# Later stages for the first weight unit, one engine for each PSUM bank of y, and T3 in front of T4: a fused attention and two-MLP kernel on one NeuronCore

## Chip, core and metric

The kernel runs on one core of a Trainium2 chip. The metric is the device time in microseconds of one execution. A profiled execution gives its own time and a span from the first to the last instruction; the sums below are made against that execution.

## What is computed

Linear attention with random features over 4 batches, 8 heads, 576 tokens of 64 values, and then two MLPs on the 2304 tokens of 512 values that the attention gives. All is float32.

```
phi(x): h = einsum('bhsd,md->bhsm', x, omega) - sum(x*x)/2 ; exp(h - max(h)) / sqrt(m)
kv  = einsum('bhsm,bhsd->bhmd', phi(k), v) ;  z = sum(phi(k), axis=2)
out = einsum('bhsm,bhmd->bhsd', phi(q), kv) / (einsum('bhsm,bhm->bhs', phi(q), z) + 1e-06)
x = out as (2304, 512)
MLP 1:  h = x @ w_in (512 x 2048);  g = max(h, 0) + alpha * min(h, 0);  x = g @ w_out
MLP 2:  h = x @ w_in (512 x 2048);  r = max(h, 0);  x = (r * r) @ w_out
```

## The kernel before, in words

**Attention.** `seq` is 18 tiles of 128 tokens of the keys and then 18 of the queries. `k_step(i)` for key tile i puts on the engines: the load of a later key and value tile (SP), the kv products of tile i-3 (TensorE, L560), the projection of tile i on omega (TensorE, L514, into a PSUM tile h, of which there are two), the sums of squares (L521), and for tile i-1 the maximum and the bias (VectorE, L527, L533, L534) and eight exponentials (ScalarE, L539, which read h). GpSimd copies the values (L604) and squares the keys (L503). So the projection of tile i writes the h that the exponentials of tile i-2 have read. Three last key steps are interleaved with the first query steps (`q_step`), which go on alone after them.

**Weights.** MLP weights come as int64 words; `Raw` loads one (L115, issued by GpSimd) and a generator, `made`, takes it in small *stages* through ScalarE scaling (`scale_high` L125, `scale_low` L128), VectorE shifts and merges (L132, L135), a GpSimd add (L137), then splits it in two float32r parts (ScalarE cast L212, VectorE rest L215), adds Strassen sums (L151) and writes the result to DRAM (`keep` L218, `keep3` L237) for later blocks, which read it back (`read`, L396). Each call of `onward` runs one stage. Weight *unit* 0 is asked for after k_step(1) (its two loads of 512 KB are issued then); from key step `MAKE_K` on, each key step ends with one stage of it, and so do the first two interleaved query steps. Stages 15 to 17 of unit 0 are empty. Later `upto` runs stages up to a number that a table names.

**MLP 1.** Three blocks of 768 tokens, each with eight *turns* (one pair of 128-column weight slices each). A turn of a block after the first does seven Strassen products (`pair`, L746) in the order 1, 2, 6, 5, 7, 4, 3, and between them, as `FILL` says, the parts of the second matmul (`mm2`, L930) of the turn before, which add into y: six PSUM banks of 512 columns, holding four pieces of 768 columns, so that banks 1 and 4 hold two pieces of 256. L771 on ScalarE makes `gh`, the rounded activation that mm2 reads, from c, which VectorE bends (L789). After a block's last mm2, `evacuate` (L948) copies y to x; this stands in the first turn of the next block, piece by piece as `COMPLETE` frees banks. At a block's end the table `NEXT` places the preparation of the next block's operands: differences T1 to T4 (L414; T1 and T3 in tile ta, T2 and T4 in tile tb), casts (ScalarE L421, xh) and rests (VectorE L424, xl). Product 7 reads T3, product 4 reads T4. MLP 2 follows with its own order.

**Order.** TensorE, VectorE, ScalarE and GpSimd execute in exactly the order in which the code issues; each is one queue, so an instruction that waits holds up all behind it. SyncE's order of transfers is chosen by the framework. Two engines that read one PSUM bank are put one after the other by the framework's semaphores.

Of the kernel before, what the change touches and what calls it, by code (L numbers as in the profile page):

```python
# [26 lines left out]
KC = DM // P  # L27
# [6 lines left out]
HB = NB // 2  # L34
NPAIR = NF // 2
QW = 2 * P
MAKE_K = 2

ZEROS = (8, 4, 4)

# [14 lines left out]
def tile_performer_moe(ctx, tc, qt, kt, qn, kn, vn, omt, w1i, w1o, al, w2i, w2o, out):  # L55
    nc = tc.nc
# [27 lines left out]
    B11, B21, B22, T4, T1, T2, T3 = range(7)  # L84
# [282 lines left out]
    def onward(most, blk):  # L367

        ask(most, blk)
        next(making[0])  # L370
# [6 lines left out]
    def ask(most, blk):  # L377

        limit[0], room[0] = most, blk
        if not making:  # L380
            making.append(made())
            next(making[0])
        fetches[0]()
# [42 lines left out]
    def as_it_is(_, n):  # L426
# [9 lines left out]
            11: [(rest, T4), (cast, B22)], 12: [(rest, B22)]},  # L436
        1: {-4: [(difference, T1)], -2: [(difference, T2)],
            1: [(cast, B11)], 2: [(rest, B11), (cast, B21)], 3: [(rest, B21), (cast, T2)],
            4: [(rest, T2), (cast, T1)], 5: [(rest, T1), (difference, T4)], 6: [(difference, T3), (cast, T4)],
            7: [(cast, T3), (rest, T4)], 8: [(rest, T3), (cast, B22)], 9: [(rest, B22)]},  # L440
    }


# [6 lines left out]
    def attention():  # L450
        with ExitStack() as ac:
# [235 lines left out]
            for i in range(NT):  # L687
                k_step(i)
                if i == 1:
                    ask(1, BLOCKS - 1)  # L690
                elif i >= MAKE_K:
                    onward(1, BLOCKS - 1)
# [243 lines left out]
    def cuts(c):  # L936

        a0 = c * NB
        while a0 < (c + 1) * NB:
            a1 = min((c + 1) * NB, (a0 // 512 + 1) * 512)  # L940
            yield a0, a1
            a0 = a1

    def evacuate(k, y, rows):

        for n, (c, a0, a1) in enumerate((c, a0, a1) for c in range(KC) for a0, a1 in cuts(c)):
            if a0 // 512 in rows:
                (nc.scalar.copy, nc.vector.tensor_copy)[n % 2](  # L948
                    out=x[:, k, c, a0 - c * NB:a1 - c * NB],
                    in_=y[a0 // 512][:, a0 % 512:a0 % 512 + a1 - a0])  # L950

# [31 lines left out]
    for n, (layer, k, turn, p) in enumerate(plan):  # L983
# [10 lines left out]
        for m, got in enumerate(steps, DRAINED if n == 0 else 0):  # L994
# [25 lines left out]
            for rows in full:  # L1020
                evacuate(ended, y, rows)
# [8 lines left out]
        for rows in full:  # L1030
            evacuate(ended, y, rows)
# [281 lines left out]
```

## Time and profile before

| | |
|---|---|
| median of 3 runs | 890.82 us (888.67 to 893.08) |
| profiled execution | 893.57 us, of which the span is 891.8 us |
| mean granted TensorE clock over the span | 0.994 |
| TensorE matmul busy | 881.9 us (99% of the span) |
| VectorE / ScalarE / GpSimd busy | 676.5 / 480.4 / 169.7 us |

How to read it: TensorE is the engine that sets the time, since it is busy almost throughout. But a busy matmul row counts a matmul at half clock as busy too, so the idle time alone does not tell what can be had. The profiled execution is 2.75 us above the median and 0.49 us above the slowest of the three runs.

### The profile page before, as it was taken

How to read it: one execution, taken by the hardware profiler on the slowest of the kernel's cores; microseconds unless marked ns; L12 is line 12 of the kernel's file. 1: busy time of each engine (PE TensorE's matmuls, PEld its weight loads, DVE VectorE, ACT ScalarE, POOL GpSimd, SP SyncE). 2: the span in 40 equal slices, each digit the busy share in tenths (PEclk: the TensorE clock that was granted, in tenths of full speed). 3: DMA queues.
4: the chain of work that ended last, by engine and by line, in shares of the span. 5: the costliest groups of instructions: out<-in, count | busy, mean ns of one | idle time of the engine just before them, and what ended most of it. 6: DMA issues, size and time to landing. Idle time of an engine off the chain costs nothing.

```text
span 891.8 us, 18473 instructions
## 1 busy us (share of the span) xinstructions
PE 881.9 (99%) x7328; PEld 837.0 (94%) x7328; DVE 676.5 (76%) x1078; ACT 480.4 (54%) x965; POOL 169.7 (19%) x192
## 2 busy tenths in 40 slices
PE   8999999999999999999999999999999999999998
PEld 5998889999998999998999999999999999999998
DVE  4767987999987778898787975668845688657674
ACT  5688886677665466475565643334523254333432
POOL 5553232444412222321323100000000000000000
PEclk9899999999999999999999999999999999999999
DMA  7445224789954899947999965767687687876763
GB/s 259 149 133 200 77 84 154 255 288 321 283 211 188 292 377 400 402 163 264 362 413 394 386 238 183 256 253 276 224 302 253 210 310 254 278 258 222 301 247 141
DMA packets 86902, 228.82 MB, mean 257 GB/s; under 512 B 6688, under 2 KB 19360, under 8 KB 81824
## 3 DMA queue, kind: packets, MB, share of 16 engines
q1 hardware_dynamic: 77248, 192.21, 59.9%
q0 software_dynamic: 9216, 33.56, 11.6%
q10 hardware_dynamic: 352, 1.87, 0.6%
q8 instruction: 58, 0.95, 0.4%
q14 instruction: 28, 0.23, 0.1%
HBM read 170.47 MB, written 57.15 MB: 255 GB/s over the span
## 4 chain that ended last, share of the span: by engine, by line
PE 54%; DVE 2%; ACT 0%; issue 0%; DVEq 0%; ACTq 0%
PE h L746 16%; PE sumb L746 10%; PE suma L1113 9%; PE sumc L1113 8%; PE y L930 8%; PE sumb L1113 3%; DVE xl L424 1%; PE h L1113 0%; DVE c L789 0%; DVE ms L215 0%; DVE c L784 0%; DVE wf L151 0%; DVE ta L414 0%; ACT gh L771 0%; DVE gl L795 0%
## 5 line engine op out<-in xcount | busy, mean ns | idle before, releaser
L746 PE MATMUL h<-xh,w 128*128 128x384 f32 x1040 | 294.7, 336 | 0.0
L746 PEld LDWEIGHTS h<-xh,w 128*128 128x128 f32 x1040 | 190.8, 188 | 2.5
L930 PE MATMUL y<-gh,w 128*128 128x512 f32 (+1 forms) x768 | 175.6, 337 | 1.4 <-ACT gh L771 1.4
L746 PE MATMUL h<-xl,w 128*128 128x384 f32 x520 | 174.7, 336 | 0.4 <-DVE xl L424 0.3
L930 PEld LDWEIGHTS y<-gh,w 128*128 128x128 f32 x768 | 131.0, 188 | 13.6 <-ACT gh L771 2.4
L137 POOL TENSOR_TENSOR wf<-x 128x512 int32<-128x512 int32 x64 | 86.2, 1347 | 240.7 <-issue 56.8
L930 PE MATMUL y<-gl,w 128*128 128x512 f32 (+1 forms) x384 | 103.4, 337 | 0.0
L746 PEld LDWEIGHTS h<-xl,w 128*128 128x128 f32 x520 | 97.7, 188 | 3.7 <-DVE xl L424 1.1
L1127 ACT CAST gh<-g 128x768 fp32r<-128x768 f32 x72 | 56.5, 831 | 81.2 <-PE suma L1113 38.9
L746 PE MATMUL sumb<-xh,w 128*128 128x384 f32 x336 | 91.3, 335 | 0.0
L1129 DVE TENSOR_TENSOR gl<-g,gh 128x768 fp32r<-128x768 f32 x72 | 65.8, 956 | 32.2 <-PE suma L1113 17.2
L930 PEld LDWEIGHTS y<-gl,w 128*128 128x128 f32 x384 | 67.5, 188 | 9.3
L771 ACT ACTIVATE gh<-c,sg_sb 128x768 fp32r<-128x768 f32 x48 | 45.0, 938 | 38.0 <-DVE c L789 37.9
L527 DVE TENSOR_REDUCE mx<-h 128x8 f32<-128x1024 f32 x36 | 44.0, 1223 | 27.8 <-PE h L514 27.3
L746 PEld LDWEIGHTS sumb<-xh,w 128*128 128x128 f32 x336 | 61.3, 188 | 0.0
L1113 PE MATMUL sumc<-w,gh 128*128 128x256 f32 x416 | 61.3, 283 | 0.0
L789 DVE SCALAR_TENSOR_TENSOR c<-c,al_sb 128x768 f32<-128x768 f32 x48 | 56.4, 1174 | 1.6 <-ACT c L771 1.6
L795 DVE SCALAR_TENSOR_TENSOR gl<-c,sg_sb,gh 128x768 fp32r<-128x768 f32 x48 | 56.6, 1181 | 1.0 <-ACT gh L771 1.0
L1113 PEld LDWEIGHTS sumc<-w,gh 128*128 128x128 f32 x416 | 56.5, 192 | 0.0
L746 PE MATMUL sumb<-xl,w 128*128 128x384 f32 x168 | 56.2, 335 | 0.0
L771 ACT ACTIVATE c<-h,sg_sb 128x384 f32<-128x384 f32 x48 | 27.8, 580 | 52.0 <-PE h L746 51.6
L1113 PE MATMUL suma<-w,gh 128*128 128x256 f32 x432 | 54.8, 283 | 0.0
(113 smaller groups left out, 1514.6 us busy)
## 6 DMA issues: line engine op xcount, KB each, us to landing
w<-k SPq DMA_DIRECT2D x99, 512.0 KB, 5.1
w<-k SPq DMA_DIRECT2D x39, 1024.0 KB, 4.8
w<-k SPq DMA_DIRECT2D x26, 896.0 KB, 9.0
k<-ms SPq DMA_DIRECT2D x36, 512.0 KB, 6.8
k<-w SPq DMA_DIRECT2D x7, 1792.0 KB, 7.5
x<-in_w1i POOLq DMA_DIRECT2D x16, 512.0 KB, 4.5
x<-in_w1o POOLq DMA_DIRECT2D x16, 512.0 KB, 4.9
k<-w SPq DMA_DIRECT2D x16, 512.0 KB, 6.9
```

The lines of the kernel that those rows point to most:

```text
L137: nc.gpsimd.tensor_tensor(out=self.out.bitcast(I32), in0=self.high, in1=self.low, op=ALU.add)
L424: nc.vector.tensor_tensor(out=tiles["xl", n], in0=of(k, n), in1=tiles["xh", n].bitcast(F32), op=ALU.subtract)
L527: nc.vector.reduce_max(out=mx, in_=pj, axis=AX.X)
L746: nc.tensor.matmul(out, w[:, u, a, cs], tiles[v, b][:, kc], start=start and kc == 0 and j == 0, stop=stop and kc == 1 and j == 2, skip_gro ...
L771: nc.scalar.mul(out=to, in_=of, mul=sg_sb[:, 2 * p + i:2 * p + i + 1])
L789: nc.vector.scalar_tensor_tensor(out=c, in0=c, scalar=slope, in1=c, op0=ALU.mult, op1=ALU.max)
L795: nc.vector.scalar_tensor_tensor(out=gl[:, i], in0=c, scalar=sign, in1=gh[:, i].bitcast(F32), op0=ALU.mult, op1=ALU.subtract)
L930: nc.tensor.matmul(y[a0 // 512][:, a0 % 512:a0 % 512 + a1 - a0], u[:, i, c * P:(c + 1) * P], v[:, i, ts], start=first and j == 0 and a0 % ...
L1113: nc.tensor.matmul(to[c], (l if v == 2 else h)[:, r, c * P:(c + 1) * P], w[:, rr, v % 2], start=fresh and rr == 0 and v == 0 and (c != 1 o ...
L1127: nc.scalar.copy(out=h[:, r], in_=f[:, r])
L1129: nc.vector.tensor_tensor(out=l[:, r], in0=f[:, r], in1=h[:, r].bitcast(F32), op=ALU.subtract)
```

## The change

Three independent edits. `MAKE_K` goes from 2 to 5: the stages of weight unit 0 follow key steps 5 to 17 and the first two query steps, where they followed key steps 2 to 17 and two query steps; the loads are asked for where they were. `evacuate` gives banks 1 and 4 (two pieces of 256 columns each) to VectorE and banks 0, 2, 3 and 5 (one piece of 512 each) to ScalarE, where it alternated by piece. In the table for blocks after the first, T3's difference, cast and rest change places with T4's.

```
-MAKE_K = 2
+MAKE_K = 5
...
-            4: [(rest, T2), (cast, T1)], 5: [(rest, T1), (difference, T4)], 6: [(difference, T3), (cast, T4)],
-            7: [(cast, T3), (rest, T4)], 8: [(rest, T3), (cast, B22)], 9: [(rest, B22)]},
+            4: [(rest, T2), (cast, T1)], 5: [(rest, T1), (difference, T3)], 6: [(cast, T3), (difference, T4)],
+            7: [(rest, T3), (cast, T4)], 8: [(rest, T4), (cast, B22)], 9: [(rest, B22)]},
...
-        for n, (c, a0, a1) in enumerate((c, a0, a1) for c in range(KC) for a0, a1 in cuts(c)):
+        for c, a0, a1 in ((c, a0, a1) for c in range(KC) for a0, a1 in cuts(c)):
             if a0 // 512 in rows:
-                (nc.scalar.copy, nc.vector.tensor_copy)[n % 2](
+                (nc.vector.tensor_copy if a0 // 512 in (1, 4) else nc.scalar.copy)(
```

First place: ScalarE in the key steps, from its first exponentials on (x8 is the set of one key tile, e the result; x<-x are the scalings of the raw weight, w<-wf the casts). Before:

```order
L539 ACTIVATE e<-h,nb 128x128 x16
L125 ACTIVATE x<-x 128x512
L539 ACTIVATE e<-h,nb 128x128 x8
L128 ACTIVATE x<-x 128x512
L539 ACTIVATE e<-h,nb 128x128 x8
L125 ACTIVATE x<-x 128x512
L539 ACTIVATE e<-h,nb 128x128 x8
L128 ACTIVATE x<-x 128x512
L539 ACTIVATE e<-h,nb 128x128 x16
L212 CAST w_0_101<-wf_99 128x512
```

And in the changed kernel, ScalarE at the same place:

```order
L539 ACTIVATE e<-h,nb 128x128 x40
L125 ACTIVATE x<-x 128x512
L539 ACTIVATE e<-h,nb 128x128 x8
L128 ACTIVATE x<-x 128x512
L539 ACTIVATE e<-h,nb 128x128 x8
L125 ACTIVATE x<-x 128x512
L539 ACTIVATE e<-h,nb 128x128 x8
L128 ACTIVATE x<-x 128x512
L539 ACTIVATE e<-h,nb 128x128 x16
L212 CAST w_0_101<-wf_99 128x512
```

The first scaling stood behind two sets of exponentials and stands behind five; the rows after it keep their order, three sets later.

Second place: ScalarE in the first turn of the third block, where y of the second leaves (y1 to y5 are banks; the difference of the two programs). At the first turns of the second block and of MLP 2 the same four rows change.

```order
 L125 ACTIVATE x_62<-x_62 128x512
 L128 ACTIVATE x_62<-x_62 128x512
-L948 COPY x_62<-y1_3968 128x256
+L948 COPY x_62<-y2_3969 128x512
 L948 COPY x_62<-y3_3970 128x512
-L948 COPY x_62<-y4_3971 128x256
+L948 COPY x_62<-y5_3972 128x512
 L771 ACTIVATE gh_5021<-c_5088,sg_sb_61 128x768
 L771 ACTIVATE s_5183<-h_5174,sg_sb_61 128x384
```

ScalarE copies 1536 columns here where it copied 1024, and no longer touches a bank of VectorE's; VectorE's four copies shrink from 256, 512, 256 and 512 columns to four of 256.

Third place: VectorE at the end of the second block (ta holds T3, tb T4; xl6 is the rest of T3, xl3 that of T4).

```order
-L414 TENSOR_TENSOR tb_2697<-x_62,tb_2697 128x768
+L414 TENSOR_TENSOR ta_2696<-x_62 128x768
 L784 SCALAR_TENSOR_TENSOR c_4892<-h_4869,sg_sb_61,s_4913 128x384
 L789 SCALAR_TENSOR_TENSOR c_4950<-c_4950,al_sb_60 128x768
 L215 TENSOR_TENSOR ma_2688<-wf1_99,ma_2688 128x256
 L151 TENSOR_TENSOR wf1_99<-wf1_99 128x256 x2
-L414 TENSOR_TENSOR ta_2696<-x_62 128x768
+L414 TENSOR_TENSOR tb_2697<-x_62,tb_2697 128x768
 L789 SCALAR_TENSOR_TENSOR c_4892<-c_4892,al_sb_60 128x768
-L424 TENSOR_TENSOR xl3_1364<-tb_2697,xh3_1363 128x768
+L424 TENSOR_TENSOR xl6_2684<-ta_2696,xh6_2683 128x768
 L784 SCALAR_TENSOR_TENSOR c_5044<-h_5024,sg_sb_61,s_5032 128x384
```

T3's rest moves up to T4's place, two instructions earlier; T4's takes T3's. TensorE's order is the same in both programs. SyncE's changes in two places: key and value loads alternate differently, and in the third block's third turn one half (896 KB) of the weights that the fourth turn reads is issued behind two stores (`keep3`) that it stood in front of.

## Rows read from the trace of the kernel before

**Rows 1.** Page, section 1: busy time of each engine.

```profile
PE 881.9 (99%) x7328; PEld 837.0 (94%) x7328; DVE 676.5 (76%) x1078; ACT 480.4 (54%) x965; POOL 169.7 (19%) x192
```

**Rows 2.** Waits of TensorE, whole span: who, for whom, us in total, times, longest.

```profile
PE h L514 <- ACT e L539: 3.3, 3, 2.9
PE y L930 <- ACT gh L771: 1.4, 3, 0.9
PE h L746 <- DVE xl L424: 0.3, 1, 0.3
```

**Rows 3.** Timeline, key steps: start, us, engine, line, operation, count, [idle before <-releaser].

```profile
15.86 0.67 ACT L125 ACTIVATE x<-x 128x512 f32<-128x512 f32 x1 [2.92 <-DMA x<-in_w1i]
18.65 1.81 PE L514 MATMUL h<-om,raw 64*128 64x128 f32 x16 [2.90 <-ACT e L539]
```

**Rows 4.** Windows: stretch, us, busy of PE, PEld, DVE, ACT, POOL, clock, DMA.

```profile
13.04:18.65 5.61, 2.71 (x69) 2.45 (x65) 2.21 (x6) 2.79 (x10) 2.52 (x4) 1.00 0.97 345
18.65:35.10 16.45, 16.45 (x289) 15.29 (x289) 9.80 (x18) 11.40 (x39) 7.72 (x9) 0.69 0.38 121
18.98:29.22 10.24, 10.24 (x140) 9.56 (x138) 4.74 (x8) 7.64 (x27) 4.42 (x5) 0.50 0.31 108
48.83:60.68 11.85, 11.85 (x288) 10.97 (x288) 8.17 (x16) 10.32 (x37) 6.98 (x10) 1.00 0.38 127
```

**Rows 5.** Timeline, two later key steps: TensorE's projections, and a ScalarE cast between.

```profile
51.47 1.16 PE L514 MATMUL h<-om,raw 64*128 64x128 f32 x16
53.91 0.67 ACT L212 CAST w<-wf 128x512 fp32r<-128x512 f32 x1
54.13 1.16 PE L514 MATMUL h<-om,raw 64*128 64x128 f32 x16
```

**Rows 6.** DMA issues from 11.6 to 11.9 us: KB, us to landing.

```profile
raw<-in_kt SPq DMA_DIRECT2D x1, 256.0 KB, 6.1
```

**Rows 7.** Timeline, y of the second block leaving, first turn of the third.

```profile
412.35 1.95 DVE L948 COPY x<-y 128x256 f32<-128x256 f32 x4
412.85 1.25 ACT L948 COPY x<-y 128x256 f32<-128x256 f32 x3 [2.31 <-DVE x L948]
413.77 0.34 PE L746 MATMUL h<-xh,w 128*128 128x384 f32 x1
414.00 0.94 ACT L771 ACTIVATE gh<-c,sg_sb 128x768 fp32r<-128x768 f32 x1
414.99 0.97 PE L930 MATMUL y<-gh,w 128*128 128x512 f32 x4 [0.88 <-ACT gh L771]
```

**Rows 8.** Timeline, the same place one block earlier.

```profile
284.68 1.25 ACT L948 COPY x<-y 128x256 f32<-128x256 f32 x3 [0.84 <-DVE x L948]
286.82 0.96 PE L930 MATMUL y<-gh,w 128*128 128x512 f32 x4 [0.29 <-ACT gh L771]
```

**Rows 9.** Groups by line and shape, 280 to 540 us: busy us, mean ns | idle.

```profile
L948 ACT COPY x<-y 128x512 f32<-128x512 f32 x6 | 3.5, 588 | 0.0
```

**Rows 10.** Timeline, second block's end: rests of T4 and T3, product 7's second matmul.

```profile
399.12 0.95 DVE L424 TENSOR_TENSOR xl<-tb,xh 128x768 fp32r<-128x768 f32 x1
401.45 0.95 DVE L424 TENSOR_TENSOR xl<-ta,xh 128x768 fp32r<-128x768 f32 x1
402.45 0.45 PE L746 MATMUL h<-xl,w 128*128 128x384 f32 x1 [0.30 <-DVE xl L424]
```

**Rows 11.** Timeline of SyncE's issues, third block's third turn.

```profile
430.26 0.46 SPq L396 DMA_DIRECT2D w<-k  x1
433.93 0.32 SPq L237 DMA_DIRECT2D k<-ma  x1
```

**Rows 12.** DMA issues from 430.2 to 430.7 us.

```profile
w<-k SPq DMA_DIRECT2D x1, 896.0 KB, 11.9
```

**Rows 13.** Chain of waits around the fourth turn's start: start, us, what.

```profile
444.64 2.08 PE h L746 x12
```

## Prediction

> **What bounds the kernel now.** I read the page first, then the waits of TensorE, then each of those waits where it stands in the timeline, and last the windows around them for the clock. TensorE's matmuls are busy for 99% of the span [rows 1], and its order is the same in both programs, so this change can win only what TensorE waits, or what it runs slowly. The view of waits gives three causes, about 5 us in all [rows 2]: the projection of a key tile behind the exponentials (3.3 us, of which 2.9 in one piece), y behind gh (1.4 us in three), and one wait of 0.3 us for a rest. Each is touched by one of the three edits.
>
> The large one is in the key steps. ScalarE stood for 2.92 us in front of the first scaling of the raw weight, until its transfer had landed at 15.86 us; the exponentials of key tile 2 were queued behind it, and TensorE waited 2.90 us for them, to 18.65 [rows 3]. The windows show what the waits do not [rows 4]: from 18.98 to 29.22 us, directly after this idle piece, the granted clock is 0.50 (1.2 GHz of 2.4), while the matmul row counts as fully busy. So 99% busy hides a loss.
>
> **The stages three steps later.** First the stall. A key step lasts 2.66 us, from projection 14 at 51.47 to projection 15 at 54.13 [rows 5]; from projection 3 to projection 4 it took 5.61 [rows 4]. Loss: 5.61 - 2.66 = 2.95 us. Then the clock. Projections 4 to 8 took 16.45 us and projections 13 to 17, whose steps hold the same matmuls (batches are 4.5 tiles, so the pattern returns after nine), took 11.85 us at full clock [rows 4]. Loss: 16.45 - 11.85 = 4.60 us. Together 7.55 us.
>
> After the change ScalarE first meets the raw weight in key step 5, behind the exponentials of tile 4. Those end shortly before projection 6, which at the regular step starts at 13.04 + 3 x 2.66 = 21.0 us, 5 us after the landing at 15.86: the wait is covered. If the cover were gone (a landing 5 us later), the stall would be back.
>
> The rule on the clock: the row says that 10.24 us at half clock, with a little around them, cost 4.60 us. The Trainium skill (TensorE: Matmul & The Clock Gate, section Terms) puts the penalty at the throttled time times one minus the granted share, which would be 10.24 x 0.5 = 5.1 us here. By that the result would be 0.5 us lower; I go by the row, since parts of a key step are not set by the clock.
>
> What is added: nothing, the stages are the same, but four scalings on four successive steps now run at full clock, where they lay beside slow matmuls. ScalarE was busy 10.32 of 11.85 us in projections 13 to 17, with two casts in it [rows 4]; with two more pieces of 0.67 us [rows 5] that is 11.66: it still fits, without room. A step with a cast in front of its exponentials lost nothing that shows (54.13 came 2.66 us after 51.47). The bounds: nothing, or all four pieces on the path, 4 x 0.67 = 2.7 us. VectorE's shifts and merges move next to other small pieces too. I take 0.3 us, near the row for small waits: of the 3.3 us the two other pieces are 0.4 us in all, over ten steps that carried such stages [rows 2]. Those two could also vanish, since the sums that stood there move; that is the upper bound, +0.4. At the end, the casts and rests of stages 13 and 14 reach the first two query steps, and stages 15 to 17 are empty, so nothing is later for unit 1. Term: 7.55 - 0.3 = 7.25 us.
>
> SyncE's loads alternate differently; the key load issued at 11.6 us landed 6.1 us later, at 17.7 [rows 6], and its projection (6) would come at 13.04 + 3 x 2.66 = 21.0: 3.3 us of cover, no cost.
>
> **One engine for each bank.** At the third block's first turn ScalarE was free at 412.85 - 2.31 = 410.54 and then waited for VectorE's copy out of the bank that the two share [rows 7]. VectorE's began only at 412.35. Behind ScalarE's three copies stood gh (414.00, 0.94 us), and y waited for it to 414.99. The last h matmul started at 413.77 and such matmuls follow each other by 2.08 / 12 = 0.17 us [rows 13], so y was late by 414.99 - 413.77 - 0.17 = 1.05 us (0.17 more than the idle 0.88, whose start is a modelled end). One block earlier the idle is 0.29 [rows 8], so by the same 0.17 late by 0.46 us.
>
> Now ScalarE does not wait there: banks 2 and 3 are full before the turn ends, bank 5 at the last y matmul, which lies twelve h matmuls before 413.94, at 411.86. Three copies of 0.59 us [rows 9], the last of them from 411.9 at the earliest, end at 412.5; gh ends at 413.4, before y is due at 413.94. The whole 1.05 goes. One block earlier ScalarE is free at 284.68 - 0.84 = 283.84 [rows 8]; 3 x 0.59 + 0.94 from there gives 286.55, and y is due at 286.82 - 0.46 = 286.36: up to 0.2 us of wait may stay. VectorE loses 512 columns of copying, which can only help what follows. Term: 1.05 + 0.35 = 1.4 us; bounds 0 (the copies wait anyway) and 1.5. At MLP 2's first turn no wait of TensorE is listed [rows 2], so 0.
>
> **T3 first.** T3's rest ended at 401.45 + 0.95 = 402.40 and product 7's second matmul began at 402.45 after 0.30 us of idle [rows 10]; with the same 0.17 it was late by 0.47. T3's rest now has T4's place at 399.12, 2.3 us earlier, and T4's, at 401.45, is needed a product and four parts of mm2 later. What waits for gh just before (the third piece of 1.4 us in [rows 2]) stays, as its queue has the same load. Term: 0.45 us; bounds 0 and 0.5.
>
> **SyncE's other change.** Half the weights of the third block's fourth turn were issued at 430.26, landed 11.9 us later at 442.2 [rows 11, 12], and the turn starts at 444.64 [rows 13]: 2.5 us of cover. In the new order they follow the store at 433.93 [rows 11], an issue later by 3.7 us. Were the landing later by all of it, TensorE would wait 1.2 us; the transfers ahead in the queue are the same but for two stores, so I take 0.
>
> **Sum.** 7.25 + 1.4 + 0.45 = 9.1 us off the profiled execution's 893.57 gives **884.5 us**. Its span is 891.8, so 1.8 us lie outside and stay. The median of the runs is 2.75 us under that execution and the fastest, 888.67, is 4.9 under it, which is about what the half clock cost it; I suppose that runs differ in this, which no row shows. Against the median of 890.82 the forecast is 0.7% less. What a measurement of this kernel can tell from no change is about 0.5%, so 886.4 and 895.3 are the borders. With the best bounds, 7.95 + 1.5 + 0.5, it is 883.6; a run as far below as the fastest of before is below its median, 882.
>
> **The rivals.**
> The clock falls anyway (0.10): key steps are made of short matmuls with small gaps, and one more half-clock stretch like the old one gives 4.6 back: 889.1, within 0.5%. For it speaks that ScalarE has no room in steps 5 to 8. Against it: from 29.22 on, with casts in the steps and the two small waits, the granted clock was 1.00 [rows 4]. The Trainium skill (TensorE: Matmul & The Clock Gate, A second HAM failure mode: psum-queue depth-cycling) says that frequent short gaps between groups of matmuls alone can make the clock go down and up; the later key steps do not bear that out here.
>
> The loads are late instead (0.06): from 13.04 to 18.65 the DMA engines were 97% busy [rows 4], and without the stall TensorE wants keys sooner. If the stall comes back whole behind a key load, it is 884.5 + 2.95 = 887.5, with the clock 892.1; no change. Against it: the 3.3 us above. The Trainium skill (DMA: Bandwidth & Descriptors, Issuing engines are not separate DMA queues) says that transfers issued by SyncE and GpSimd share the same 16 engines and interleave, so the 1 MB of weights does delay the keys; the row of 6.1 us has that in it.
>
> The copies do not part (0.05): all write the tile x, and if ScalarE is still held by VectorE there, 1.4 stays: 885.9, still faster.
>
> Slower (0.05): the clock falls at about 19 us and the key steps, too sparse at half speed to raise it, keep it to their end. A microsecond at half clock costs 4.60 / 10.24 = 0.45 us. The upper border is reached at (895.3 - 884.5) / 0.45 = 24 us of it; from 19 us to the end of the key steps at about 60.7 - 7.5 = 53 it would be 34 us: 884.5 + 15.3 = 899.8. Against it: the old stretch ended by itself after 10.24 us.
>
> **How the numbers follow.** The forecast has 0.74; its own range is 882 to 886.4. Together with the copies' case that is 0.79; to hold 8 in 10 the range takes in the milder half of the late loads: 882.0 to 888.0. Faster by over 0.5%: 0.74 less 0.05 for runs of it above 886.4, and 0.04 of the copies' case, 0.73. Within 0.5%: the clock, the loads and the rest, 0.22. Slower: 0.05.
>
> **What would show it.** The first scaling starts at once behind exponentials, near 21 us, with no wait for its transfer; the projections 3 to 8 take 14.5 us or so instead of 22.06, with a clock of 1.00 throughout; the waits of the projection fall from 3.3 to under 0.8 us. At the two block starts no ScalarE copy waits for VectorE and gh is done before TensorE comes. The wait for xl at product 7 is gone, and none for T4 takes its place. A granted clock of 0.50 anywhere between 6 us and the end, or a key or weight transfer as a releaser of TensorE, would make me wrong.

## Result: 884.45 us, 0.7% less

The changed kernel takes 884.45 us (median of 12 runs, 883.85 to 888.21 without the one named below), the kernel before 890.84 (12 runs, 887.05 to 898.55). The medians are 6.4 us apart, 0.7%; the ratio on record for the runs compared is 0.9919, 95% interval 0.9894 to 0.9945, so the fall is clear of the noise. One run of the changed kernel, 1218.66 us at a mean granted clock of 0.654, is left out of the comparison; it was the profiled one, so the profile after is that of a second run of the same kernel (884.69 us, its span 882.9; label after_again below).

Cores and page of the profile after:

```profile
core 0: 882.9 us, clock 1.000
...
PE 877.0 (99%) x7328; PEld 832.9 (94%) x7328; DVE 673.6 (76%) x1078; ACT 481.0 (54%) x965; POOL 169.6 (19%) x192
```

Waits of TensorE after (who, for whom, us in total, times, longest):

```profile
PE t L508 <- DVE pick L483: 1.2, 1, 1.2
PE h L514 <- ACT e L539: 0.6, 2, 0.3
PE y L930 <- ACT gh L771: 0.4, 1, 0.4
```

Against [rows 2], the projection waits 0.6 us where it waited 3.3, y 0.4 where it waited 1.4, and the wait for xl is gone. (The first row is TensorE's own start, before any data.) TensorE's busy time fell by 4.9 us, from 881.9 [rows 1] to 877.0, with the same 7328 matmuls: for the most part that is the half clock, which the row counts as work.

Timeline after, key steps: projections 3 to 8 and the first scaling (start, us, engine, line, operation, count):

```profile
12.98 1.16 PE L514 MATMUL h<-om,raw 64*128 64x128 f32 x16
...
15.62 1.28 PE L514 MATMUL h<-om,raw 64*128 64x128 f32 x16
...
18.38 1.16 PE L514 MATMUL h<-om,raw 64*128 64x128 f32 x16
...
20.80 0.74 ACT L125 ACTIVATE x<-x 128x512 f32<-128x512 f32 x1
...
21.02 1.16 PE L514 MATMUL h<-om,raw 64*128 64x128 f32 x16
...
23.75 1.16 PE L514 MATMUL h<-om,raw 64*128 64x128 f32 x16
...
27.57 0.60 PE L514 MATMUL h<-om,raw 64*128 64x128 f32 x6
```

The scaling starts at 20.80 with no wait in its row; in [rows 3] it started at 15.86 after 2.92 us. The same stretch as a window (length, busy of PE, PEld, DVE, ACT, POOL, clock, DMA):

```profile
12.98:27.57 14.59, 14.59 (x356) 13.54 (x353) 9.81 (x22) 13.12 (x47) 8.59 (x12) 1.00 0.85 276
```

Projections 3 to 8 take 14.59 us at a clock of 1.00, where they took 5.61 + 16.45 = 22.06 [rows 4]. ScalarE is busy 13.12 of 14.59 us: it fits, as the prediction had it, without room.

Two small waits are left, before projections 12 and 13:

```profile
38.52 1.16 PE L514 MATMUL h<-om,raw 64*128 64x128 f32 x16 [0.31 <-ACT e L539]
...
41.49 1.16 PE L514 MATMUL h<-om,raw 64*128 64x128 f32 x16 [0.26 <-ACT e L539]
```

The same two projections waited in the kernel before, a little less:

```profile
45.95 1.16 PE L514 MATMUL h<-om,raw 64*128 64x128 f32 x16 [0.19 <-ACT e L539]
...
48.83 1.16 PE L514 MATMUL h<-om,raw 64*128 64x128 f32 x16 [0.16 <-ACT e L539]
```

Timeline after, the third block's first turn, where y of the second leaves (answers to [rows 7]):

```profile
403.95 0.59 ACT L948 COPY x<-y 128x512 f32<-128x512 f32 x1 [0.53 <-PE y L930]
...
404.26 1.41 DVE L948 COPY x<-y 128x256 f32<-128x256 f32 x4
...
404.44 0.94 ACT L771 ACTIVATE gh<-c,sg_sb 128x768 fp32r<-128x768 f32 x1
...
405.69 0.34 PE L746 MATMUL h<-xh,w 128*128 128x384 f32 x1
...
405.86 0.40 PE L930 MATMUL y<-gh,w 128*128 128x512 f32 x1
```

ScalarE's last copy waits for TensorE to fill bank 5, no longer for VectorE, whose copies start 0.31 us after it. gh ends at 405.38, y follows the last h matmul by 0.17 us, the regular distance: nothing is late. The Trainium skill (PSUM — Partial Sum Buffer, PSUM bank collisions raise a hardware error) says that the compiler's scheduler orders any two engines that touch the same bank and quadrant, reads against reads too. This trace agrees: with no bank in common, ScalarE's row names VectorE no more, and the two copy at the same time.

One block earlier (answers to [rows 8]):

```profile
278.16 0.96 ACT L771 ACTIVATE gh<-c,sg_sb 128x768 fp32r<-128x768 f32 x1
...
278.83 0.34 PE L746 MATMUL h<-xh,w 128*128 128x384 f32 x1
...
279.18 0.96 PE L930 MATMUL y<-gh,w 128*128 128x512 f32 x4
```

Here gh ends at 279.12, and y begins 0.35 us after the last h matmul where 0.17 is regular: 0.18 us are left, of the "up to 0.2" that the prediction allowed.

The second block's end, T3's rest and T4's, and the y that waits just before (answers to [rows 10]):

```profile
389.94 0.96 PE L930 MATMUL y<-gh,w 128*128 128x512 f32 x4 [0.38 <-ACT gh L771]
...
391.63 0.96 DVE L424 TENSOR_TENSOR xl<-ta,xh 128x768 fp32r<-128x768 f32 x1
...
393.20 0.41 PE L746 MATMUL h<-xh,w 128*128 128x384 f32 x1
...
393.45 0.34 PE L746 MATMUL h<-xl,w 128*128 128x384 f32 x1
...
393.95 0.96 DVE L424 TENSOR_TENSOR xl<-tb,xh 128x768 fp32r<-128x768 f32 x1
```

T3's rest ends at 392.59, 0.86 us before product 7 reads it at 393.45, without idle. The third of the y waits stays, as the prediction said, but it grew from the 0.25 us of the kernel before:

```profile
397.43 0.97 PE L930 MATMUL y<-gh,w 128*128 128x512 f32 x4 [0.25 <-ACT gh L771]
```

This comes with T3's edit: of the traces with a mean clock over 0.99, the nine that have T3 in front show 0.38 or 0.39 us here, the four others 0.25 to 0.27. So about 0.13 us of what that edit wins is given back; the prediction had taken it that this queue's load stays the same.

### The profile page after: what moved, and what is told of

The parts are those of the page before. It is cut to its first block, busy times and chain, and to the rows that moved or that the text cites. A ratio compares the mean times of both kernels' runs of the same rounds, so it can differ in the third digit from the quotient of the medians.

```text
span 1216.9 us, 18475 instructions
## 1 busy us (share of the span) xinstructions
PE 1212.2 (100%) x7328; PEld 1041.0 (86%) x7328; DVE 665.8 (55%) x1078; ACT 481.0 (40%) x965; POOL 167.2 (14%) x192
## 4 chain that ended last, share of the span: by engine, by line
PE 100%; DVE 0%; issue 0%
PE h L746 31%; PE y L930 23%; PE sumb L746 10%; PE suma L1113 9%; PE sumc L1113 8%; PE h L514 4%; PE sumb L1113 3%; PE o L560 2%; PE t L521 2%; PE t L634 2%; PE o L666 2%; PE t L653 1%; PE t L508 1%; PE h L1113 0%; DVE x L1268 0%; DVE zeros L674 0%
## 5 line engine op out<-in xcount | busy, mean ns | idle before, releaser
L746 PE MATMUL h<-xh,w 128*128 128x384 f32 x1040 | 380.4, 425 | 0.0
L746 PEld LDWEIGHTS h<-xh,w 128*128 128x128 f32 x1040 | 214.9, 207 | 40.5 <-issue 2.0
L930 PE MATMUL y<-gh,w 128*128 128x512 f32 (+1 forms) x768 | 235.5, 425 | 0.0
L746 PE MATMUL h<-xl,w 128*128 128x384 f32 x520 | 220.3, 424 | 0.0
L930 PEld LDWEIGHTS y<-gh,w 128*128 128x128 f32 x768 | 155.0, 214 | 40.3 <-issue 9.2
L930 PE MATMUL y<-gl,w 128*128 128x512 f32 (+1 forms) x384 | 134.1, 424 | 0.0
L746 PEld LDWEIGHTS h<-xl,w 128*128 128x128 f32 x520 | 109.6, 211 | 22.2 <-issue 1.8
L746 PE MATMUL sumb<-xh,w 128*128 128x384 f32 x336 | 118.6, 424 | 0.0
L1127 ACT CAST gh<-g 128x768 fp32r<-128x768 f32 x72 | 56.5, 832 | 131.7 <-PE suma L1113 65.4
L784 DVE SCALAR_TENSOR_TENSOR c<-h,sg_sb,s 128x384 f32<-128x384 f32 x48 | 29.6, 618 | 99.4 <-PE h L746 69.8
L1113 PE MATMUL sumc<-w,gh 128*128 128x256 f32 x416 | 82.3, 343 | 0.0
L746 PEld LDWEIGHTS sumb<-xh,w 128*128 128x128 f32 x336 | 69.2, 207 | 13.3
L1113 PEld LDWEIGHTS suma<-w,gh 128*128 128x128 f32 x432 | 72.3, 253 | 0.0
L746 PE MATMUL sumb<-xl,w 128*128 128x384 f32 x168 | 71.3, 424 | 0.0
```

Source lines behind the costliest of these rows:

```text
L746: nc.tensor.matmul(out, w[:, u, a, cs], tiles[v, b][:, kc], start=start and kc == 0 and j == 0, stop=stop and kc == 1 and j == 2, skip_gro ...
L784: nc.vector.scalar_tensor_tensor(out=c[:, ts], in0=b, scalar=sign, in1=s, op0=ALU.mult, op1=ALU.add)
L930: nc.tensor.matmul(y[a0 // 512][:, a0 % 512:a0 % 512 + a1 - a0], u[:, i, c * P:(c + 1) * P], v[:, i, ts], start=first and j == 0 and a0 % ...
L1113: nc.tensor.matmul(to[c], (l if v == 2 else h)[:, r, c * P:(c + 1) * P], w[:, rr, v % 2], start=fresh and rr == 0 and v == 0 and (c != 1 o ...
L1127: nc.scalar.copy(out=h[:, r], in_=f[:, r])
```

## Experiments

Twelve kernels ran, in four sets; each set has its own chip and its own runs of the kernel before. The first four ask what the parts are worth and whether the stall and the clock are the cause. The later ones follow from what the runs of the kernel before showed on the way: they are not alike.

### The parts, and the stall alone

**The changed kernel again** (no edit).

> The changed kernel once more, for a profile at the full granted clock. My theory (A): the early stages cost a stall of 2.95 us and, behind it, 4.60 us of half clock; the copies 1.4, the order of T3 and T4 0.45. Then 884.5 us, projections 3 to 8 in about 14.5 us at a granted clock of 1.00, waits of the projection under 0.8 us. Rival (B), that the scalings themselves slow the key steps and not the clock: projections 5 to 9 of the changed kernel, which carry the four scalings, take about as long as the old 16.45 us. Rival (C), that the copies and T3 give most of it: the key steps gain under 3 us.

Measured: 885.71 us (12 runs, 884.69 to 886.58) beside 891.54 (35 runs, 886.83 to 899.49), ratio 0.9939 (0.9918 to 0.9960). Its trace is shown above.

**Later stages alone.**

```
-MAKE_K = 2
+MAKE_K = 5
```

> MAKE_K = 5 alone. A: 7.25 us of the 9.1, so 886.3 us, 0.994 of the kernel before against a profiled execution of it, and 1.85 us above the whole change; the waits of y for gh (1.4 us) and of product 7 (0.3 us) stand as before. B and C: within 3 us of the kernel before.

Measured: 887.61 (12 runs, 886.55 to 889.95), ratio 0.9963 (0.9941 to 0.9986). Waits of TensorE in it:

```profile
PE h L514 <- ACT e L539: 0.6, 2, 0.3
...
PE h L746 <- DVE xl L424: 0.3, 1, 0.3
```

The wait for xl stands as before, and y's three too (1.4 us). It is 1.90 us above the whole change: that is what copies and T3 are worth (the prediction's 1.85). The median lies 1.3 us above the 886.3 expected, and 3.9 under the kernel before, where rivals B and C had less than 3.

**Copies and T3 without the later stages** (`MAKE_K = 2`, the rest as changed).

> The copies by bank and T3 in front, with MAKE_K = 2 as before. A: 1.85 us off, 889 to 891.7 us according to how much of the time at half clock an execution has; the stall of 2.9 us is there, and the profile shows about 10 us at a granted clock of 0.50 behind it. Executions with a mean clock near 0.999 should be some 4.6 us shorter than those near 0.994. C: 884 to 886 us.

Measured: 889.59 (12 runs, 885.54 to 892.13), ratio 0.9966 (0.9937 to 0.9995). The first scaling and the window behind the stall:

```profile
15.32 0.67 ACT L125 ACTIVATE x<-x 128x512 f32<-128x512 f32 x1 [2.78 <-DMA x<-in_w1i]
...
18.08:24.90 6.82, 6.79 (x80) 6.24 (x80) 2.50 (x4) 5.88 (x19) 2.63 (x3) 0.50 0.23 85
```

Stall and half clock are back (6.82 us of it, where about 10 were expected). But its runs fall into two groups: five at a mean granted clock of 0.999 or 1.000 took 885.54 to 886.68 us, as the changed kernel does; seven at 0.994 to 0.996 took 889.50 to 892.13. The kernel before shows the same: of its 35 runs, eight have a mean clock of 1.000 and took 886.83 to 888.13, the other 27 have 0.987 to 0.998 and took 889.21 to 899.49. So the loss in the key steps is there in most executions and absent in some. The eight are as fast as the runs of stages_only at a mean clock of 1.000 (886.55 to 888.20): where the clock does not fall, the later stages win nothing that these times show.

**The stall filled** (the kernel before, with 13 matmuls of zeros ahead of projection 4, so that TensorE does not stand idle; they compute nothing that is used).

```
-            def idle(n):
+            def idle(n, to=1):
...
-                    nc.tensor.matmul(tt[1][:, H:], zeros[:, 0:P], zeros[:, H:], start=True, stop=True)
+                    nc.tensor.matmul(tt[to][:, H:], zeros[:, 0:P], zeros[:, H:], start=True, stop=True)
...
                 if has(i):
+                    if i == 4:
+                        idle(13, 0)
```

> The kernel before, with thirteen matmuls on zeros (0.2 us each, results never read) in front of the projection of key tile 4, where TensorE idled 2.9 us; nothing else is changed, so ScalarE still waits for the weight and the projection still comes at about 18.7 us. A: the stall of 2.95 us stays, but the clock does not fall (1.00 from 6 us on), projections 4 to 8 take 11.9 to 12.3 us in place of 16.45, and the execution is some 4.6 us shorter than the profiled one of before: 889 us. B: projections 4 to 8 still take about 16 us, since the scalings are there, and the time is that of the kernel before, 890 to 893.6.

Measured: 889.65 (12 runs, 888.99 to 891.58), ratio 0.9978 (0.9953 to 1.0004). Timeline:

```profile
14.07 0.68 ACT L125 ACTIVATE x<-x 128x512 f32<-128x512 f32 x1 [0.81 <-DMA x<-in_w1i]
...
14.64 2.16 ACT L539 ACTIVATE e<-h,nb 128x128 f32<-128x128 f32 x8
...
16.00 2.94 PE L508 MATMUL t<-zeros 128*128 128x504 bf16 x13
...
18.86 1.16 PE L514 MATMUL h<-om,raw 64*128 64x128 f32 x16
```

The median fell by less than 2 us, since the zeros take their 2.94 us in every execution. But the clock stayed at 0.999 or 1.000 in all 12 runs, and their spread shrank to 2.6 us from the 12.7 of the kernel before. With the scalings where they were, work in place of TensorE's idle time was enough to keep the clock up: the fall comes with the stall, not with the scalings. It is the clocks of the 12 runs that show this, not the trace: in the traced execution the transfer landed early, ScalarE waited 0.81 us and not 2.92, and the exponentials that projection 4 needs ended at 16.80, so that the zeros stood for about 0.8 us of idle time and the rest of them came on top. Whether less work in that place would do was not tried. The second thing in these rows was not asked for: the landing varies.

### Is it the landing?

A new theory, D: the stall is what the transfer is late by when ScalarE comes to it, the landing varies between executions, and the clock falls behind a stall only. Then it is the distance between request and first scaling that counts, not the key step.

**Stages after key step 3** (as changed, `MAKE_K = 3`).

> The changed kernel with the stages after key step 3, one step later than in the kernel before. ScalarE came to the first scaling at 12.94 us in the kernel before and at 20.80 in the changed one, so it comes here at about 15.6. The first weight transfer landed at 15.86, 15.30 and 14.05 us in three traces whose scaling stood after key step 2. Theory D (the stall is what the landing is late by, and the clock falls only behind a stall): a wait of 0 to 0.3 us, the clock at 1.00 from 6 us on, and the time of the changed kernel, 885.7 to 886.3, with a spread of its runs under 4 us. Rival B (what costs is scalings that lie among the first key steps, wherever the transfer is): two of three steps are given back, so two thirds of the 3.9 us between the changed kernel (885.71) and the one without later stages (889.59), 888.3, with a half-clock stretch in the trace.

Measured: 884.95 (6 runs, 884.43 to 886.55) beside 891.55 (17 runs, 886.80 to 895.16), ratio 0.9922 (0.9898 to 0.9945). The first scaling in its timeline:

```profile
15.86 0.72 ACT L125 ACTIVATE x<-x 128x512 f32<-128x512 f32 x1
```

No wait, and nothing given back: 3.3 us under rival B's 888.3. One of the six runs (886.55) has a mean clock of 0.998.

**Stages after key step 4** (`MAKE_K = 4`).

> The changed kernel with the stages after key step 4. Theory D: the scaling comes at about 18.2 us, behind any landing seen, so 885.7, the changed kernel's time. It could be up to 0.7 lower, 885.0: the two new waits of 0.38 and 0.33 us before the projections at 38.5 and 41.5 us stand where a rest of the weight and the copy of a batch's kv fall into one key step of VectorE, and they meet in another step here. Rival B: one third of the 3.9 us is given back, 887.0.

Measured: 884.92 (6 runs, 884.23 to 889.35), ratio 0.9926 (0.9898 to 0.9953). Again all of it; the two small waits became one of 0.5 us, and the run of 889.35 has a clock of 0.996, so a later stage makes the fall rare, not impossible. Whether TensorE stood idle in that run, no trace shows.

**Asked for earlier, scalings where they were** (`MAKE_K = 2`, copies and T3 as changed).

```
-                if i == 1:
+                if i == 0:
                     ask(1, BLOCKS - 1)
```

> The kernel with the copies by bank and T3 first, the stages after key step 2 as before, but the two weight loads asked for one key step earlier (after step 0). Theory D: the issue comes 2.7 us earlier; if the landing moves as much, to 11.4 to 13.2 us, ScalarE at 12.94 waits 0.3 us at most, the clock stays at 1.00 and the time is 885.9, what the runs of the kernel with late loads gave when their clock was 1.00 (885.54 to 886.68). If the transfers of keys and values slow it and it moves by 1 us only, stalls of 0.1 to 1.9 us are left, and the time lies between 886 and 889. Rival B: scalings at the same place cost the same, 889.6, clock 0.996.

Measured: 884.63 (6 runs, 884.03 to 885.01, each at a clock of 1.000), ratio 0.9915 (0.9891 to 0.9938). GpSimd's issue and the first scaling:

```profile
7.08 0.72 POOL L115 DMA_DIRECT2D x<-in_w1i  x1
...
12.74 0.72 ACT L125 ACTIVATE x<-x 128x512 f32<-128x512 f32 x1
```

This decides between D and B: the scaling comes 3.1 us earlier than in [rows 3], waits for nothing, and the time is that of the changed kernel. The issue came 1.9 us earlier than in the kernel before (7.08 and 9.01), not 2.7 as expected, and that was enough.

**Asked for later** (`MAKE_K = 3`, the request after step 2: the scalings one step later than before, about as far from the request as before).

```
-                if i == 1:
+                if i == 2:
                     ask(1, BLOCKS - 1)
```

> The kernel with the stages after key step 3, which lost nothing, but with its two weight loads asked for after step 2 and no longer after step 1. The scalings stand one step later than in the kernel before, as far from the request as there. Theory D: the issue comes at 11.7 instead of 9.1 us; with the 4.8 to 6.8 us that the first transfer took in the traces so far it lands at 16.5 to 18.5, ScalarE at 15.6 waits for it 0.9 to 2.9 us, and the clock falls behind that in most executions: 887 to 889.5, spread 4 us or more. Rival E (the first transfer is late only because of what else is loaded near 9 us, or the place of the scalings decides): no wait, clock 1.00, 885.0, as with the request after step 1.

Measured: 887.02 (12 runs, 883.28 to 894.30) beside 891.21 (29 runs, 887.07 to 898.38), ratio 0.9958 (0.9929 to 0.9988). Its issue, its first scaling and the window at half clock:

```profile
10.58 0.72 POOL L115 DMA_DIRECT2D x<-in_w1i  x1
...
16.71 0.69 ACT L125 ACTIVATE x<-x 128x512 f32<-128x512 f32 x1 [1.70 <-DMA x<-in_w1i]
...
21.02:24.42 3.40, 3.40 (x52) 3.28 (x52) 1.88 (x4) 3.40 (x14) 2.29 (x3) 0.50 0.34 93
```

The stall, the half clock and the spread of 11 us are back, with scalings at the step that had lost nothing above. The median is at the lower edge of what D expected, and 1.9 us above the exchanged engines below (885.10), which ran beside it; eight of the 12 runs have a clock of 0.998 or less, none of the ten with exchanged engines. One run of 889.70 has a clock of 1.000, so the half clock is not what cost it its time. The issue came at 10.58 us, not at the 11.7 expected; ScalarE was there 4.4 us after it, where it was 3.9 after it in the kernel before.

**Early request and late stages together** (the request after step 0, `MAKE_K = 4`).

> The two settings that did best put together: the weight loads asked for after key step 0, the stages after key step 4, copies and T3 as in the changed kernel. Theory D: the first transfer lands near 12 us and its scaling comes near 18, so the cover is over 5 us; no stall is left to be won, and what remains over the changed kernel is the two waits of 0.7 us that the stages after step 4 do not have: 884.3, every run at clock 1.00, spread under 3 us. Rival E (an earlier request takes room from the keys that TensorE wants at 10 to 18 us, which the earlier run at this request did not show because its own stages were earlier too): a wait for keys and 885.5 or more.

Measured: 884.91 (12 runs, 883.99 to 889.61) beside 891.35 (17 runs), ratio 0.9936 (0.9907 to 0.9966). The 0.6 us expected below the changed kernel did not come: the trace has one wait of 0.5 us for the exponentials. All 12 runs have a clock of 0.999 or 1.000, but the spread is 5.6 us and not under 3. The run of 889.61 has that clock too, so something else cost it over 4 us, which no trace shows.

### The copies and T3, one at a time

**Copies by bank alone** (the edit of `evacuate` on the kernel before).

> Only the copies by bank. TensorE's waits of y for gh fall from 1.4 us in three to 0.4 in one, the wait of 0.3 us for a rest before product 7 stays, and the half clock of the key steps too when their first scaling stalls. By the sum of the prediction 1.4 us below the kernel before at the same clock: 890.1 beside 891.5. If the copies give nothing (their time comes back in VectorE's or ScalarE's queue), 891.5; if they give all of what copies and T3 gave together, 889.6.

Measured: 890.06 (10 runs, 885.64 to 896.68), ratio 0.9987 (0.9958 to 1.0015): between "nothing" and "all", not told apart from no change by time. The trace tells more: y waits 0.7 us in two pieces (1.4 in three before; the 0.4 expected was too low). The piece that was not expected is the y one block earlier, in the timeline:

```profile
279.49 0.68 ACT L125 ACTIVATE x<-x 128x512 f32<-128x512 f32 x1 [2.06 <-DMA x<-in_w2i]
...
283.05 0.96 PE L930 MATMUL y<-gh,w 128*128 128x512 f32 x4 [0.42 <-ACT gh L771]
```

ScalarE's copies no longer wait for VectorE there, but they stand behind a scaling that waited 2.06 us for its weight. In the kernel before that wait is 1.27 us and in the changed kernel's trace 1.63. stages_at_3 has 2.06 and the wait of y too, so at this block the gain depends on a landing as well. With the engines exchanged (below), ScalarE stood 2.00 us, copied for 1.17 us in place of 1.54, and y was not late.

And a shorter stall in the key steps, in the timeline and the window behind it:

```profile
15.00 0.71 ACT L125 ACTIVATE x<-x 128x512 f32<-128x512 f32 x1 [1.80 <-DMA x<-in_w1i]
...
19.54:22.94 3.40, 3.40 (x48) 3.28 (x46) 1.63 (x4) 3.40 (x14) 2.54 (x3) 0.50 0.32 91
```

**T3 first alone** (the edit of the table on the kernel before).

> Only T3 in front of T4. The wait of 0.3 us before product 7 goes and the three of y (1.4 us) stay: 0.45 us under the kernel before at the same clock. Rival: T4's rest is waited for in its place, no gain. In the key steps everything stands as in the kernel before; theory D: the wait of ScalarE at the first scaling is the landing of the transfer less about 13 us, and a half-clock stretch follows where that is 1 us or more.

Measured: 892.52 (10 runs, 888.32 to 899.95), ratio 1.0021 (0.9986 to 1.0055): inconclusive, 0.45 us is far below what these runs tell. Its trace has no wait for xl, the y waits at 1.6 us, and the longest stall of all (timeline, and the window behind it):

```profile
16.31 0.66 ACT L125 ACTIVATE x<-x 128x512 f32<-128x512 f32 x1 [3.33 <-DMA x<-in_w1i]
...
19.08:25.91 6.83, 6.83 (x82) 6.26 (x82) 2.50 (x4) 5.84 (x19) 2.63 (x3) 0.50 0.21 60
```

**Engines exchanged** (as changed, but ScalarE takes banks 1 and 4).

```
-                (nc.vector.tensor_copy if a0 // 512 in (1, 4) else nc.scalar.copy)(
+                (nc.scalar.copy if a0 // 512 in (1, 4) else nc.vector.tensor_copy)(
```

> The changed kernel with the two engines exchanged in the copies of y: ScalarE takes the four pieces of 256 columns (banks 1 and 4), VectorE the four of 512. Each bank is still left by one engine, but VectorE copies 2048 columns at each of the three places, where it copied 1024 in the changed kernel and 1536 in the kernel before. If what counts is that ScalarE does not wait for VectorE's copy of a shared bank, ScalarE still waits for none, gh is made in time, y waits 0.4 us in all and the time stays at that of the changed kernel, 885.2 (within 0.5). If what counted was VectorE's lighter queue, h and the bent c come later behind the larger copies: the waits of y or of h for VectorE are back with 1 us or more, 886.6 and up.

Measured: 885.10 (10 runs, 883.94 to 886.11), ratio 0.9922 (0.9896 to 0.9947). y waits once, 0.4 us, though VectorE copies 2048 columns at each place. What counts is that no bank is shared, not that VectorE has less to copy.

## Why the prediction was right

**The stall and the clock.** The mechanism is shown from five sides: stall_filled (with work in the place of the idle time the clock stays up), ask_early and stages_at_3 (with distance to the landing there is no stall), ask_late (without distance it comes back), and the changed kernel itself. That the clock falls behind a stall only, as theory D says, is not shown (see the rivals below). The price holds too. In five traces the key steps, from the first projection to the first transposition of the queries, are longer than the 56.5 us of four kernels without a stall (56.48 to 56.60) by about the wait plus 0.45 us for each us at half clock, the prediction's 4.60 / 10.24:

| kernel | ScalarE's wait, us | clock 0.50 for, us | key steps, us | over 56.5 | wait + 0.45 x half clock |
|---|---|---|---|---|---|
| before | 2.92 | 10.24 | 63.94 | 7.4 | 7.5 |
| t3_only | 3.33 | 6.83 | 62.82 | 6.3 | 6.4 |
| copies_and_t3 | 2.78 | 6.82 | 61.95 | 5.4 | 5.8 |
| copies_only | 1.80 | 3.40 | 60.04 | 3.5 | 3.3 |
| ask_late | 1.70 | 3.40 | 59.22 | 2.7 | 3.2 |

(The four are after_again, stages_only, ask_early and early_and_4.) The first row is the trace from which the 0.45 was taken, so the other four are the test. Three more traces have no stall and lie less close: stages_at_4 takes 56.21 us, stages_at_3 56.68, and banks_swapped 57.76, where projection 2 came 6.3 us after the first and not 5.4 to 5.7, and a wait of 0.35 us within projection 4 has no releaser in the profile. Counted from projection 3, which leaves out the start, all seven take 47.85 to 48.78 us, and the five of the table are over 48.2 by 7.4, 6.2, 5.7, 3.2 and 3.0: within 0.2 us of the last column.

From trace to trace the term is 63.94 - 56.60 = 7.34 us, where 7.25 was forecast; the whole came to 893.57 - 884.69 = 8.88 us from one profiled execution to the other, where the sum was 9.1. As a share of the medians it is 3.9 us (stages_only against before, and the whole change against copies_and_t3). Both are right, because the profiled execution of before was a dear one; the prediction set its sum against that execution's 893.57 and not against the median, and supposed "that runs differ in this, which no row shows". Had it taken 9.1 us off the median, it would have said 881.7, 2.7 us too low. That the forecast met the median to 0.05 us is luck: the same kernel's median was 885.71 in the next set. And the lower end of the range, 882, let the changed kernel's runs spread as those of before did, although the forecast took away the half clock from which most of that spread came; the fastest run was 883.85.

**The small waits** in the fuller steps: 0.6 us in two, where the same two projections waited 0.4 before; a loss of 0.2, of the 0.3 taken. That the fuller steps cause it was not tested by itself.

**Copies and T3.** 1.85 us forecast; 1.90 by time (stages_only less after_again). By the trace, from the first row of TensorE's L746 to its last one (MLP 1 and most of MLP 2; timeline), the kernel before:

```profile
136.91 0.42 PE L746 MATMUL h<-xh,w 128*128 128x384 f32 x1
...
829.69 0.33 PE L746 MATMUL sumb<-xh,w 128*128 128x384 f32 x1
```

The same rows of copies_only:

```profile
133.01 0.42 PE L746 MATMUL h<-xh,w 128*128 128x384 f32 x1
...
824.76 0.33 PE L746 MATMUL sumb<-xh,w 128*128 128x384 f32 x1
```

Of t3_only:

```profile
135.79 0.42 PE L746 MATMUL h<-xh,w 128*128 128x384 f32 x1
...
828.07 0.33 PE L746 MATMUL sumb<-xh,w 128*128 128x384 f32 x1
```

Of the changed kernel:

```profile
129.55 0.42 PE L746 MATMUL h<-xh,w 128*128 128x384 f32 x1
...
820.84 0.33 PE L746 MATMUL sumb<-xh,w 128*128 128x384 f32 x1
```

That is 692.78, 691.75, 692.28 and 691.29 us. Single traces do not give the parts: stages_only and stall_filled, whose MLPs are those of before, take 693.75 and 693.23, up to 1 us more than before, and the seven other kernels with both edits 690.69 to 691.27. But all eight with both edits lie under all three with neither, by 2.2 us in the mean (691.0 and 693.25), and the two with one edit lie between. So the traces give about 2 us for the two terms together, and the times 1.9. How they divide is shown by the waits alone. Of the copies' 1.4 us, the 1.05 at the third block went in every trace with that edit; of the 0.35 one block earlier, none came in copies_only and stages_at_3. T3's wait went in every trace with that edit, less the 0.13 that came back at the y before it, so its 0.45 is too high rather than too low.

**SyncE's order** at nothing: no transfer is among the waits of TensorE after.

**The rivals.** The copies part (banks_swapped too). The loads were not late. The clock did not fall in the trace above, but two runs of the changed kernel in the first comparison (887.06 and 888.21 us) have a mean of 0.998, one of stages_only (889.95) has 0.996, and stages_at_3 and stages_at_4 have one each (0.998 and 0.996): what that rival describes happens in single runs. None of these was traced, so whether their clock fell behind a late landing or without any stall stays open. The long half clock did not come in the runs compared; what held the one left out at a mean clock of 0.654 is open.

## What to carry to other kernels

A wait for a transfer in a stage of short matmuls can cost more than its own length, as the five stalls of 1.70 to 3.33 us did here: look at the granted clock behind it, and price the stretch at the later, regular steps. Before a sum is set against a median, look whether the runs of the kernel before fall into groups by their mean clock: a term read from one execution may be missing in a quarter of them, and what the edit then buys is part of the term in the median (3.9 of 7.3 us here) and a smaller spread. Asking for the data one step earlier did the same here as using it three steps later.

## What the runs showed of the hardware

The same 512 KB, issued by GpSimd at the same time within 0.02 us (8.99, 9.00 and 9.01 us in copies_only, t3_only and the kernel before), was there at 15.00, 16.31 and 15.86 us; in stall_filled at 14.07. That spread of 2.2 us, with DMA engines nearly full in this stretch (0.97 in [rows 4]), decides how long the stall is.

The stretches at half clock behind a stall lasted 3.40 (twice), 6.82, 6.83 and 10.24 us, and not in the order of the stalls (1.80, 1.70, 2.78, 3.33, 2.92). TensorE had unbroken work in them (busy 10.24 of 10.24 us in [rows 4]), so being busy did not end the half clock at once. Not every wait was followed by one: y stood 0.88 us for gh in the third block [rows 7], and the clock stayed at its upper level there. Why the length differs stays open.
